# Single-query attention over 8192 keys: one loop over all pairs of heads on TensorE, VectorE and ScalarE

## Chip, cores and metric

The kernel runs on one core of a Trainium2 chip. The metric is device time in microseconds (us); lower is better. The time before is 321.45 us, the median of 3 runs (321.19 to 321.46).

## What is computed

Sixteen heads, one query per head, 8192 keys and values of 256 numbers each, all bf16. The softmax goes over the 8192 scores of a head.

```python
B, H, Sq, Sk, D = 1, 16, 1, 8192, 256
def reference(q, k, v):
    scale = q.shape[-1] ** -0.5
    scores = jnp.einsum("bhqd,bhkd->bhqk", q, k) * scale
    p = _softmax(scores, axis=-1)
    return jnp.einsum("bhqk,bhkd->bhqd", p, v)
```

## The kernel before

**Layout.** A head's K is 128 x 64 x 256: partition p holds keys 64p to 64p+63, as 64 columns of 256 numbers (`J` = 64). V lies the same way. One head of K or of V is 4096 KB. There are two buffers for K, two for V (`kbuf`, `vbuf`, by the parity of the head), and two each of scores `S`, exponents `E`, the query copy `q_now` and the accumulator `acc`.

**SyncE** (L124 to L140) issues all transfers from a list, in the order k(h+2), v(h), k(h+3), v(h+1) and so on. K of head h waits until VectorE (semaphore `kd`) and TensorE (`tp`) have read K of head h-2; V of head h waits for the products of head h-2 (`pv`). The first K comes in 16 and 48 columns; V of head 13 comes in halves, of head 14 in chunks of 16 columns, of head 15 in chunks of 16, 16, 12, 8, 6, 4 and 2 (`V_LATE`).

**VectorE** (L165) makes 48 of a head's 64 scores per partition, one multiply-and-add per column (`tensor_tensor_reduce`, L186). Then it takes the row maximum over all 64 columns, `m` (L203). In between it does two small steps for the head before: `xmax` (L169) reduces the 128 maxima, which TensorE has transposed into `mx`, to one number `g`; `recips` (L174) inverts the sum of exponents. `xmax` runs after column 11 (`xmax_at=11`). Head 0 and head 15 are written apart from the loop, and head 15 is called with `xmax_at=0`. A head starts when its K has landed, its query copy is there (`qb`), and the exponents of the head two back have been taken (`ex`).

**TensorE** (L214) makes the other 16 scores. `scores(t)` is, in this order: `transpose_m` of head t-1 (L218: row maxima to one row); four groups, each of `ktrans` (L278: 8 transposes of K to `tp`) and, one group later, `kscore` (L292: 8 products with the query, from the copy `KT` that ScalarE makes of `tp`); after `ktrans` of group 1 and `kscore` of group 0, `bcast` of head t-1 (L224: `g` to all partitions, waits for VectorE's L169); at the end `total` of head t-1 (L234: sum of the exponents). `pv(h)` is 64 products of a column of exponents with a column of V (L244), summed in `acc`; I call it P·V. Outside the loop stand the scores of heads 0 and 1; the loop does scores(t), pv(t-2) for t = 2 to 15, two heads a turn; behind it `pv_late` does P·V of 14 and 15 chunk by chunk, and in that of 14 the three small matmuls of head 15 come after 32, 48 and 64 products.

**ScalarE** (L353) is unrolled over the heads. For head t: the result of head t-3 (`final`, L394, and the output transfer), four copies `KT` (L368), after the first of them the query copy of head t+1 (`q_copy`, L359), after the second `expo` of head t-1 (L376 negates the broadcast maximum, L380 takes the exponents), at the end `scopy` (L372: TensorE's scores to `S`).

**GpSimd** makes two identity matrices and two rows of ones at the start.

Every engine runs its instructions in order; the order above is the one written in the code. In a loop turn a semaphore's awaited value comes from the turn's number (`_Step.of`).

Of the kernel before, what the change touches and what calls it, by code (L numbers as in the profile page):

```python
# [15 lines left out]
V_LATE = {14: (16, 16, 16, 16), 15: (16, 16, 12, 8, 6, 4, 2)}  # L16


class _Step:
# [10 lines left out]
    def back(self, n):  # L30
        return _Step(self.c - n, self.i)
# [6 lines left out]
def bass_standalone__mha_softmax__decode_kernel(nc: bass.Bass, q: bass.AP, k: bass.AP, v: bass.AP, out: bass.AP):  # L38
# [15 lines left out]
    stream = [("k", 0, 0, K_FIRST, "k00"), ("k", 0, K_FIRST, J, "k0"), ("k", 1, 0, J, "k1")]  # L54
    stream += [("v", 0, 0, HALF, "va0"), ("k", 2, 0, J, "k0"), ("v", 0, HALF, J, "va0")]
    stream += [("v", 1, 0, HALF, "va1"), ("k", 3, 0, J, "k1"), ("v", 1, HALF, J, "va1")]
    for h in range(2, H):
        if h + 2 < H:
            stream.append(("k", h + 2, 0, J, f"k{h % 2}"))
        if h in V_LATE:  # L60
            c = 0
            for i, s in enumerate(V_LATE[h]):
                stream.append(("v", h, c, c + s, f"v{h}_{i}"))
                c += s
        elif h == V_HALVED:
            stream += [("v", h, 0, HALF, f"va{h % 2}"), ("v", h, HALF, J, f"vb{h % 2}")]
        else:
            stream.append(("v", h, 0, J, f"va{h % 2}"))

    with contextlib.ExitStack() as ctx:  # L70
# [17 lines left out]
        q_all = sb("q_all", [P, H * QW], dt)  # L88
# [24 lines left out]
        for name in ("l", "rc", "pv", "fin", "ldq", "k00", "k0", "k1", "va0", "va1", "vb0", "vb1", "o0", "o1"):  # L113
            sem(name)
        for h, sizes in V_LATE.items():
            for i in range(len(sizes)):
                sem(f"v{h}_{i}")
# [4 lines left out]
        if True:  # L122

            @(lambda f: f(nc.sync))  # L124
            def _(sp):
                for kind, h, a, b, name in stream:
                    buf = (kbuf if kind == "k" else vbuf)[h % 2]
                    if h >= 2 and a == 0:
                        if kind == "k":
                            sp.wait_ge(sem("kd"), h - 1)  # L130
                            sp.wait_ge(sem("tp"), (h - 1) * NG)
                        else:
                            sp.wait_ge(sem("pv"), h - 1)
                    sp.dma_start(  # L134
                        buf[:, a * D : b * D], src(k if kind == "k" else v, h)[:, a * D : b * D]
                    ).then_inc(sem(name), 16)
                    if kind == "v" and b == J and h not in V_LATE and h != V_HALVED:

                        sp.nop().then_inc(sem(f"vb{h % 2}"), 16)
# [3 lines left out]
            def _(pool):  # L143
# [19 lines left out]
                pool.memset(ones_col[:, :], 1.0).then_inc(sem("cf"), 1)  # L163

            @(lambda f: f(nc.vector))  # L165
            def _(dve):
                def xmax(h):
                    dve.wait_ge(sem("mT"), h.of(1, 1))
                    dve.tensor_reduce(g[0:1, h.par : h.par + 1], mx[0:1, 0:P], AX.X, ALU.max).then_inc(sem("g"), 1)  # L169

                def recips(h):
                    dve.wait_ge(sem("l"), h.of(1, 1))
                    dve.wait_ge(sem("fin"), h.of(1, 1))
                    dve.reciprocal(recip[0:1, h.par : h.par + 1], mx[0:1, P : P + 1]).then_inc(sem("rc"), 1)  # L174

                def head(h, first=False, xmax_at=11):
                    dve.wait_ge(sem("qb"), h.of(1, 1))
                    dve.wait_ge(sem("ex"), h.of(1, 0) if not first else 1)
                    buf = kbuf[h.par]
                    for j in range(JD):  # L180
                        if first and j == 0:
                            dve.wait_ge(sem("k00"), 16)
                        if j == (K_FIRST if first else 0):

                            dve.wait_ge(sem(f"k{h.par}"), h.of(8, 16 - 8 * h.par))  # L185
# [10 lines left out]
                        if j == xmax_at and not first:  # L196
                            xmax(h.back(1))
                    ins.then_inc(sem("kd"), 1)
                    if not first:
                        recips(h.back(1))  # L200
                    dve.wait_ge(sem("kd"), h.of(1, 1))
                    dve.wait_ge(sem("sc"), h.of(1, 1))
                    dve.tensor_reduce(m[:, h.par : h.par + 1], S[h.par][:, :], AX.X, ALU.max).then_inc(sem("m"), 1)  # L203
# [11 lines left out]
            def _(pe):  # L215
                def transpose_m(h):
                    pe.wait_ge(sem("m"), h.of(1, 1))
# [4 lines left out]
                def bcast(h):  # L222
                    pe.wait_ge(sem("g"), h.of(1, 1))
# [8 lines left out]
                def total(h):  # L232
                    pe.wait_ge(sem("ex"), h.of(1, 2))
                    pe.matmul(  # L234
                        mx[0:1, P : P + 1],
# [6 lines left out]
                def products(h, a, b):  # L242
                    for j in range(a, b):
# [7 lines left out]
                    if b == J:  # L251
                        ins.then_inc(sem("pv"), 1)

                def pv(h):
                    pe.wait_ge(sem("fin"), h.of(1, 1))

                    for a, name, more in ((0, "va", 16), (HALF, "vb", 0)):
                        pe.wait_ge(sem(f"{name}{h.par}"), h.of(8, 16 + more - 8 * h.par))
                        products(h, a, a + HALF)

                def pv_late(h, between):
                    pe.wait_ge(sem("fin"), h.of(1, 1))
                    a = 0
                    for i, s in enumerate(V_LATE[h.c]):
                        pe.wait_ge(sem(f"v{h.c}_{i}"), 16)
                        products(h, a, a + s)
                        a += s
                        if i in between:
                            between[i]()

                def ktrans(h, gi):
                    buf = kbuf[h.par]
                    if gi == 0:
                        pe.wait_ge(sem(f"k{h.par}"), h.of(8, 16 - 8 * h.par))
                    for b in range(GRP):
# [9 lines left out]
                def kscore(h, gi, first):  # L285
                    pe.wait_ge(sem("kt"), h.of(NG, gi + 1))
                    if gi == 0 and not first:
                        pe.wait_ge(sem("sc"), h.of(1, 0))
# [12 lines left out]
                def scores(t, first=False):  # L301
                    if not first:
                        transpose_m(t.back(1))
                    for gi in range(NG):
                        ktrans(t, gi)
                        if gi >= 1:
                            kscore(t, gi - 1, first)
                        if gi == 1 and not first:
                            bcast(t.back(1))
                    kscore(t, NG - 1, first)  # L310
                    if not first:
                        total(t.back(1))
# [25 lines left out]
                pe.wait_ge(sem("cf"), 3)  # L338
# [12 lines left out]
                pv_late(last, {})  # L351

            @(lambda f: f(nc.scalar))  # L353
            def _(act):
                def q_copy(h):
                    if h >= 2:
                        act.wait_ge(sem("kd"), h - 1)
                        act.wait_ge(sem("sp"), (h - 1) * NG)
                    act.activation(  # L359
                        out=q_now[h % 2][:, :], in_=q_all[:, h * QW : (h + 1) * QW], func=ACT.Copy  # L360
                    ).then_inc(sem("qb"), 1)

                def evac(h, gi):
                    n = h * NG + gi
                    act.wait_ge(sem("tp"), n + 1)
                    if n >= 2:
                        act.wait_ge(sem("sp"), n - 1)
                    act.activation(out=KT[gi % 2][:, :], in_=tp[gi % 2][:, :], func=ACT.Copy).then_inc(sem("kt"), 1)  # L368

                def scopy(h):  # L370
                    act.wait_ge(sem("sp"), (h + 1) * NG)
                    act.activation(out=S[h % 2][:, JD:J], in_=spe[:, 0:NPE], func=ACT.Copy).then_inc(sem("sc"), 1)  # L372

                def expo(h):
                    act.wait_ge(sem("bc"), h + 1)
                    act.activation(  # L376
                        out=negb[:, h % 2 : h % 2 + 1], in_=sm[:, 0:1], func=ACT.Copy, scale=-1.0
                    ).then_inc(sem("nb"), 1)
                    act.wait_ge(sem("nb"), h + 1)
                    act.activation(  # L380
                        out=E[h % 2][:, :],
                        in_=S[h % 2][:, :],
                        func=ACT.Exp,
                        bias=negb[:, h % 2 : h % 2 + 1],
                        scale=1.0,
                        accum_out=lsum[:, h % 2 : h % 2 + 1],
                    ).then_inc(sem("ex"), 1)

                def final(h):
                    act.wait_ge(sem("rc"), h + 1)  # L390
                    act.wait_ge(sem("pv"), h + 1)
                    if h >= 2:
                        act.wait_ge(sem(f"o{h % 2}"), 16 * (h // 2))
                    act.activation(  # L394
                        out=o_sb[h % 2][0:1, :],
                        in_=acc[h % 2][0:1, 0:D],
                        func=ACT.Copy,
                        scale=recip[0:1, h % 2 : h % 2 + 1],
                    ).then_inc(sem("fin"), 1)
                    act.wait_ge(sem("fin"), h + 3)  # L400
# [68 lines left out]
```

## Time and profile before

| | |
|---|---|
| median of 3 runs | 321.45 us |
| the profiled execution | 320.95 us |
| its span on the core | 319.5 us |
| VectorE busy | 274.4 us |
| TensorE matmuls busy | 225.7 us |
| ScalarE busy | 93.0 us |
| HBM read | 134.23 MB |
| mean granted TensorE clock | 0.829 |

All views below come from the profiled execution. PE is TensorE's matmuls, PEld its weight loads, DVE is VectorE, ACT ScalarE, POOL GpSimd, SPq the queue of SyncE. A row of the timeline has the start in us from the span's start, the length, the engine, the line (L186 is line 186 of the kernel before), the instruction, out<-in, how many stand in the row, and in brackets the engine's idle time before and what ended it. A row of a table of stretches has the stretch, its length, busy time of each engine with the number of instructions, then the granted clock (1.00 is full), the mean busy share of the 16 DMA engines, and GB/s. Where one line stands out of its view, "..." is above or below it.

### The profile page before, as it was taken

What the parts mean: (1) busy time and instruction counts of PE and PEld (TensorE: products, weight loads), DVE (VectorE), ACT (ScalarE), POOL (GpSimd) and SP (SyncE); (2) the same over time, 40 slices, a digit from 0 to 9 for tenths busy, and PEclk for the clock granted to TensorE, in tenths of its full rate; (3) what the DMA queues carried; (4) which work ended last, traced back from release to release, by engine and by line L of the source; (5) the groups of instructions that cost most, each with busy time, mean ns of one, the idle gap of its engine ahead of it and who ended that gap; (6) DMA issues with size and microseconds to landing.
All of it is one profiled execution on the core that took longest, in us unless ns stands there. A gap on an engine that the chain in (4) does not pass through costs nothing.

```text
span 319.5 us, 6525 instructions
## 1 busy us (share of the span) xinstructions
PE 225.7 (71%) x2162; PEld 161.9 (51%) x2162; DVE 274.4 (86%) x1584; ACT 93.0 (29%) x170; POOL 1.3 (0%) x10
## 2 busy tenths in 40 slices
PE   3627059788795958668585793957759577597997
PEld 1325045556564645546454563744546445465774
DVE  1999999999999999797997979989797997969910
ACT  4525132333315060330603314042330603305010
POOL 1000000000000000000000000000000000000000
PEclk9999999969687885969669597885957859697899
DMA  8999999999999999999999999999999999999994
GB/s 329 451 401 443 401 457 412 406 438 435 423 451 410 443 439 423 435 419 451 414 443 435 423 443 410 451 424 431 439 419 451 414 439 439 419 418 418 424 415 183
DMA packets 6553, 134.34 MB, mean 421 GB/s; under 512 B 752, under 2 KB 912, under 8 KB 1424
## 3 DMA queue, kind: packets, MB, share of 16 engines
q1 hardware_dynamic: 6480, 134.22, 98.3%
q8 instruction: 4, 0.07, 0.1%
q14 instruction: 5, 0.04, 0.0%
q10 hardware_dynamic: 64, 0.02, 0.0%
HBM read 134.23 MB, written 0.01 MB: 420 GB/s over the span
## 4 chain that ended last, share of the span: by engine, by line
DVE 50%; DMA 40%; PE 5%; issue 3%; ACT 1%; DVEq 0%; SPq 0%; ACTq 0%
DVE kbuf L186 48%; DMA kbuf<-in_k_dram 37%; PE acc L244 5%; DMA vbuf<-in_v_dram 3%; DVE S L186 2%; ACT KT L368 1%; DVE g L169 1%; SPq L134 0%; PE tp L278 0%; ACT o_sb L394 0%; PE spe L292 0%; DVE recip L174 0%; DVEq L206 0%; DVEq L185 0%; ACT E L380 0%
## 5 line engine op out<-in xcount | busy, mean ns | idle before, releaser
L186 DVE CUSTOM_DVE_ANT_0 kbuf<-kbuf,q_now 128x256 bf16<-128x256 bf16 x768 | 267.8, 411 | 30.2 <-DMA kbuf<-in_k_dram 22.4
L244 PE MATMUL acc<-vbuf,E 128*1 128x256 bf16 x1024 | 146.1, 315 | 14.5 <-DMA vbuf<-in_v_dram 14.4
L244 PEld LDWEIGHTS acc<-vbuf,E 128*1 128x1 bf16 x1024 | 97.4, 96 | 59.7 <-issue 14.9
L368 ACT ACTIVATE KT<-tp 128x1024 bf16<-128x1024 bf16 x64 | 64.4, 1020 | 30.4 <-PE tp L278 30.0
L186 DVE DVE_READ_ACCUMULATOR2_ANT S<- 128x1 f32 x768 | 56.4, 73 | 0.0
L394 ACT ACTIVATE o_sb<-acc,recip 1x256 bf16<-1x256 f32 x16 | 7.4, 464 | 153.5 <-PE acc L244 152.3
L278 PE MATMUL tp<-identb,kbuf 128*128 128x128 bf16 x512 | 46.2, 252 | 5.6 <-DMA kbuf<-in_k_dram 5.6
L278 PEld LDWEIGHTS tp<-identb,kbuf 128*128 128x128 bf16 x512 | 36.3, 113 | 10.4 <-DMA kbuf<-in_k_dram 5.3
L292 PE MATMUL spe<-q_now,KT 128*128 128x1 bf16 x512 | 23.6, 167 | 24.0 <-ACT KT L368 23.6
L292 PEld LDWEIGHTS spe<-q_now,KT 128*128 128x128 bf16 x512 | 19.4, 104 | 32.1 <-ACT KT L368 32.1
L224 PE MATMUL sm<-g,ones_row 1*128 1x1 f32 x32 | 7.1, 288 | 28.1 <-DVE g L169 28.1
L224 PEld LDWEIGHTS sm<-g,ones_row 1*128 1x128 f32 x32 | 5.7, 221 | 29.6 <-DVE g L169 29.3
L218 PE MATMUL mx<-ident,m 128*1 128x128 f32 x32 | 6.5, 288 | 13.9 <-DVE m L203 13.9
L376 ACT ACTIVATE negb<-sm 128x1 f32<-128x1 f32 x16 | 2.7, 172 | 28.9 <-PE sm L224 28.9
L218 PEld LDWEIGHTS mx<-ident,m 128*1 128x1 f32 x32 | 2.5, 84 | 14.8 <-DVE m L203 14.1
L359 ACT ACTIVATE q_now<-q_all 128x258 bf16<-128x258 bf16 x16 | 6.5, 410 | 0.0
L329 PE MATMUL acc<-q_sb,identb 16*128 16x256 bf16 x16 | 4.4, 403 | 2.3 <-ACT q_all L415 2.3
L169 DVE TENSOR_REDUCE g<-mx 1x1 f32<-1x128 f32 x16 | 4.4, 274 | 1.9 <-PE mx L218 1.9
L380 ACT ACTIVATE E<-S,negb 128x64 bf16<-128x64 f32 x16 | 5.6, 348 | 0.5
L174 DVE RECIPROCAL recip<-mx 1x1 f32<-1x1 f32 x16 | 2.4, 152 | 3.7 <-PE mx L234 3.7
L372 ACT ACTIVATE S<-spe 128x16 f32<-128x16 f32 x16 | 2.9, 183 | 7.5 <-PE spe L292 7.5
L415 ACT ACTIVATE q_all<-acc 128x512 bf16<-128x512 f32 x8 | 4.4, 592 | 0.6 <-PE acc L329 0.6
(19 smaller groups left out, 15.7 us busy)
## 6 DMA issues: line engine op xcount, KB each, us to landing
kbuf<-in_k_dram SPq DMA_DIRECT2D x15, 4096.0 KB, 21.9
vbuf<-in_v_dram SPq DMA_DIRECT2D x11, 4096.0 KB, 29.2
vbuf<-in_v_dram SPq DMA_DIRECT2D x6, 2048.0 KB, 24.0
vbuf<-in_v_dram SPq DMA_DIRECT2D x6, 1024.0 KB, 14.6
kbuf<-in_k_dram SPq DMA_DIRECT2D x1, 3072.0 KB, 11.6
kbuf<-in_k_dram SPq DMA_DIRECT2D x1, 1024.0 KB, 4.7
vbuf<-in_v_dram SPq DMA_DIRECT2D x1, 768.0 KB, 10.9
vbuf<-in_v_dram SPq DMA_DIRECT2D x1, 512.0 KB, 11.7
```

What stands on the lines that cost most here:

```text
L169: dve.tensor_reduce(g[0:1, h.par : h.par + 1], mx[0:1, 0:P], AX.X, ALU.max).then_inc(sem("g"), 1)
L186: ins = dve.tensor_tensor_reduce(out=buf[:, j * D : (j + 1) * D], in0=buf[:, j * D : (j + 1) * D], in1=q_now[h.par][:, 0:D], scale=SCALE, ...
L218: pe.matmul(mx[0:1, 0:P], lhsT=m[:, h.par : h.par + 1], rhs=ident[:, :], start=True, stop=True).then_inc(sem("mT"), 1)
L224: pe.matmul(sm[:, 0:1], lhsT=ones_row[0:1, 0:P], rhs=g[0:1, h.par : h.par + 1], start=True, stop=True,).then_inc(sem("bc"), 1)
L244: ins = pe.matmul(acc[h.par][0:1, 0:D], lhsT=E[h.par][:, j : j + 1], rhs=vbuf[h.par][:, j * D : (j + 1) * D], start=(j == 0), stop=(j == J ...
L278: ins = pe.transpose(tp[gi % 2][:, b * D + hf * P : b * D + (hf + 1) * P], buf[:, j * D + hf * P : j * D + (hf + 1) * P], identb[:, :],)
L292: ins = pe.matmul(spe[:, c : c + 1], lhsT=KT[gi % 2][:, b * D + hf * P : b * D + (hf + 1) * P], rhs=q_now[h.par][:, D + hf : D + hf + 1], ...
L329: ins = pe.matmul(acc[pair % 2][:, (h % 2) * D : (h % 2 + 1) * D], lhsT=identb[0:H, h : h + 1].to_broadcast([H, P]), rhs=q_sb[:, :], start ...
L359: act.activation(out=q_now[h % 2][:, :], in_=q_all[:, h * QW : (h + 1) * QW], func=ACT.Copy).then_inc(sem("qb"), 1)
L368: act.activation(out=KT[gi % 2][:, :], in_=tp[gi % 2][:, :], func=ACT.Copy).then_inc(sem("kt"), 1)
L380: act.activation(out=E[h % 2][:, :], in_=S[h % 2][:, :], func=ACT.Exp, bias=negb[:, h % 2 : h % 2 + 1], scale=1.0, accum_out=lsum[:, h % 2 ...
L394: act.activation(out=o_sb[h % 2][0:1, :], in_=acc[h % 2][0:1, 0:D], func=ACT.Copy, scale=recip[0:1, h % 2 : h % 2 + 1],).then_inc(sem("fin ...
```

## The change

The three engines get one loop each, over all eight pairs of heads (TensorE has nine turns). What the first and last turns lack or need is told by branches on the turn's number and by semaphores that GpSimd counts up at the start (`AHEAD`, and 16 or 32 on some of the transfers' semaphores). `ev` and `od` are the even and odd head of a turn, `old` or `prev` is the odd head of the turn before.

- VectorE: head `ev` runs `xmax` of `prev` after column 40; head `od` runs `recips` of `prev` after column 8, `xmax` of `ev` after column 11 and `recips` of `ev` at its end. What concerns `prev` stands in a branch. There is no head written apart.
- TensorE: a turn is scores(ev) without the small matmuls, P·V of the even head of the turn before with the small matmuls of `old` after 32, 48 and 64 products, scores(od) with those of `ev`, P·V of `old`. Each part stands in a branch. Every P·V has the waits at the chunk borders of heads 14 and 15; the value awaited rises with the last turn. `total` writes to `qps` in place of `mx`.
- ScalarE: a loop of eight turns with two heads. `expo` of the odd head of the turn before comes behind `scopy` of the even head; `final` of head t-2 comes at the end of head t, in a branch. `q_copy` copies head t+1 for all t, so for a head 16 too, whose query is set to zero (`q_all` is longer by one head). `expo` of 15 and `final` of 14 and 15 stand behind the loop.
- SyncE: the same transfers in the same order; awaited values are shifted by what is counted up, and the no-ops behind whole V transfers go.

```diff
+AHEAD = {"kd": 1, "sc": 1, "sp": 2, "ex": 2, "m": 1, "g": 1, "mT": 1, "l": 1, "bc": 1, "nb": 1, "rc": 2, "pv": 2, "fin": 4}
+V_SEMS = (("va0", "v0b", "v0c", "v0d"), ("va1", "v1b", "v1c", "v1d", "v1e", "v1f", "v1g"))
...
                         if kind == "k":
-                            sp.wait_ge(sem("kd"), h - 1)
+                            sp.wait_ge(sem("kd"), h)
                             sp.wait_ge(sem("tp"), (h - 1) * NG)
                         else:
-                            sp.wait_ge(sem("pv"), h - 1)
+                            sp.wait_ge(sem("pv"), h + 1)
...
-                        sp.nop().then_inc(sem(f"vb{h % 2}"), 16)
...
+                pool.memset(q_all[:, H * QW : (H + 1) * QW], 0.0).then_inc(sem("cf"), 1)
+                for name, n in AHEAD.items():
+                    pool.nop().then_inc(sem(name), n)
...
-                head(_Step(0), first=True)
-                with dve.Fori(0, (H - 2) // 2) as i:
-                    head(_Step(1, i))
-                    head(_Step(2, i))
+                with dve.Fori(0, H // 2) as i:
+                    ev, od = _Step(0, i), _Step(1, i)
+                    prev = od.back(2)
+
+                    def later(f):
+                        with dve.If(i > 0):
+                            f(prev)
+
+                    head(ev, {40: lambda: later(xmax)})
+                    head(od, {8: lambda: later(recips), 11: lambda: xmax(ev), JD: lambda: recips(ev)})
                 last = _Step(H - 1)
-                head(last, xmax_at=0)
                 xmax(last)
                 recips(last)
...
-                scores(_Step(0), first=True)
-                scores(_Step(1))
-                with pe.Fori(0, (H - 2) // 2) as i:
-                    for c in (2, 3):
-                        t = _Step(c, i)
-                        scores(t)
-                        pv(t.back(2))
-                last = _Step(H - 1)
-                pv_late(
-                    last.back(1),
-                    {1: lambda: transpose_m(last), 2: lambda: bcast(last), 3: lambda: total(last)},
-                )
-                pv_late(last, {})
+                with pe.Fori(0, H // 2 + 1) as i:
+                    ev, od = _Step(0, i), _Step(1, i)
+                    fin_turn = pe.snap((i // 8) * 16 + 16)
+                    half_turn = pe.snap(((i + 1) // 8) * 16 + 16)
+                    old = od.back(2)
+                    with pe.If(i < H // 2):
+                        scores(ev)
+                    with pe.If(i > 0):
+                        pv(
+                            ev.back(2),
+                            {V_LATE[14][n]: [(V_SEMS[0][n], fin_turn)] for n in range(1, len(V_SEMS[0]))},
+                            {32: lambda: transpose_m(old), 48: lambda: bcast(old), 64: lambda: total(old)},
+                        )
+                    with pe.If(i < H // 2):
+                        scores(od, before=ev)
+                    with pe.If(i > 0):
+                        waits = {V_LATE[15][n]: [(V_SEMS[1][n], fin_turn)] for n in range(1, len(V_SEMS[1]))}
+                        waits[HALF].append(("v1h", half_turn))
+                        pv(old, waits, {})
...
-                for t in range(H):
-                    if t >= 3:
-                        final(t - 3)
-                    for gi in range(NG):
-                        evac(t, gi)
-                        if gi == 1 and t >= 1:
-                            expo(t - 1)
-                        if gi == 0 and 1 <= t < H - 1:
-                            q_copy(t + 1)
-                    scopy(t)
-                final(H - 3)
-                expo(H - 1)
-                final(H - 2)
-                final(H - 1)
+                with act.Fori(0, H // 2) as i:
+                    for c in (0, 1):
+                        t = _Step(c, i)
+                        evac(t, 0)
+                        act.wait_ge(sem("kd"), t.of(1, 1))
+                        act.wait_ge(sem("sp"), t.of(NG, 2))
+                        q_copy(_Step(c + 1, i), q_all[:, bass.ds(i * (2 * QW) + (c + 1) * QW, QW)])
+                        evac(t, 1)
+                        if c:
+                            expo(t.back(1))
+                        evac(t, 2)
+                        evac(t, 3)
+                        scopy(t)
+                        with act.If(i > 0):
+                            if c == 0:
+                                expo(t.back(1))
...
+                            final(done, flat[:, bass.ds(at, D)])
+                expo(_Step(H - 1))
+                for h in (H - 2, H - 1):
+                    final(_Step(h), out[0, h, 0:1, :])
```

More of the change, by code (lines that the diff above doesn't have):

```diff
@@ L112, in bass_standalone__mha_softmax__decode_kernel @@
             sem(name)
-        for name in ("l", "rc", "pv", "fin", "ldq", "k00", "k0", "k1", "va0", "va1", "vb0", "vb1", "o0", "o1"):
+        for name in ("l", "rc", "pv", "fin", "ldq", "k0", "k0b", "k1", "va0", "va1", "v1h", "o0", "o1"):
             sem(name)
-        for h, sizes in V_LATE.items():
-            for i in range(len(sizes)):
-                sem(f"v{h}_{i}")
+        late = [name for row in V_SEMS for name in row[1:] if name not in ("v0c", "v1c")] + ["v1h"]
+        for row in V_SEMS:
+            for name in row[1:]:
+                sem(name)
         def src(t, h):
@@ L167, in xmax, with head @@
                 def xmax(h):
-                    dve.wait_ge(sem("mT"), h.of(1, 1))
+                    dve.wait_ge(sem("mT"), h.of(1, 2))
                     dve.tensor_reduce(g[0:1, h.par : h.par + 1], mx[0:1, 0:P], AX.X, ALU.max).then_inc(sem("g"), 1)
                 def recips(h):
[L172 to L176, printed above, removed]
+                    dve.wait_ge(sem("l"), h.of(1, 2))
+                    dve.wait_ge(sem("fin"), h.of(1, 3))
+                    dve.reciprocal(recip[0:1, h.par : h.par + 1], qps[0:1, 0:1]).then_inc(sem("rc"), 1)
+                def head(h, at):
                     dve.wait_ge(sem("qb"), h.of(1, 1))
-                    dve.wait_ge(sem("ex"), h.of(1, 0) if not first else 1)
+                    dve.wait_ge(sem("ex"), h.of(1, 1))
+                    dve.wait_ge(sem(f"k{h.par}"), h.of(8, 16 - 8 * h.par))
                     buf = kbuf[h.par]
                     for j in range(JD):
[L181 to L185, printed above, removed]
+                        if j == K_FIRST and h.par == 0:
+                            dve.wait_ge(sem("k0b"), 16)
                         ins = dve.tensor_tensor_reduce(
@@ L195, in head @@
                         )
-                        if j == xmax_at and not first:
-                            xmax(h.back(1))
+                        if j in at:
+                            at[j]()
                     ins.then_inc(sem("kd"), 1)
[L199 to L202, printed above, removed]
+                    if JD in at:
+                        at[JD]()
+                    dve.wait_ge(sem("kd"), h.of(1, 2))
+                    dve.wait_ge(sem("sc"), h.of(1, 2))
                     dve.tensor_reduce(m[:, h.par : h.par + 1], S[h.par][:, :], AX.X, ALU.max).then_inc(sem("m"), 1)
-                head(_Step(0), first=True)
-                with dve.Fori(0, (H - 2) // 2) as i:
-                    head(_Step(1, i))
-                    head(_Step(2, i))
+                with dve.Fori(0, H // 2) as i:
[6 more added lines that the diff above has]
+                    head(od, {8: lambda: later(recips), 11: lambda: xmax(ev), JD: lambda: recips(ev)})
                 last = _Step(H - 1)
-                head(last, xmax_at=0)
                 xmax(last)
@@ L240, in total, with pv @@
                     ).then_inc(sem("l"), 1)
-                def products(h, a, b):
-                    for j in range(a, b):
+                def pv(h, waits, at):
+                    pe.wait_ge(sem("fin"), h.of(1, 3))
+                    pe.wait_ge(sem(f"va{h.par}"), h.of(8, 32 - 8 * h.par))
+                    for j in range(J):
+                        for name, value in waits.get(j, ()):
+                            pe.wait_ge(sem(name), value)
                         ins = pe.matmul(
@@ L250, in products @@
                         )
[L251 to L269, printed above, removed]
+                        if j == J - 1:
+                            ins.then_inc(sem("pv"), 1)
+                        if j + 1 in at:
+                            at[j + 1]()
                 def ktrans(h, gi):
@@ L283, in ktrans, with kscore @@
                     ins.then_inc(sem("tp"), 1)
-                def kscore(h, gi, first):
+                def kscore(h, gi):
                     pe.wait_ge(sem("kt"), h.of(NG, gi + 1))
-                    if gi == 0 and not first:
-                        pe.wait_ge(sem("sc"), h.of(1, 0))
+                    if gi == 0:
+                        pe.wait_ge(sem("sc"), h.of(1, 1))
                     for b in range(GRP):
@@ L299, in kscore, with scores @@
                     ins.then_inc(sem("sp"), 1)
-                def scores(t, first=False):
-                    if not first:
-                        transpose_m(t.back(1))
+                def scores(t, before=None):
+                    if before:
+                        transpose_m(before)
                     for gi in range(NG):
@@ L306, in scores @@
                         if gi >= 1:
[L307 to L312, printed above, removed]
+                            kscore(t, gi - 1)
+                        if gi == 1 and before:
+                            bcast(before)
+                    kscore(t, NG - 1)
+                    if before:
+                        total(before)
                 pe.wait_ge(sem("ldq"), 16)
@@ L353, in _, with q_copy @@
             @(lambda f: f(nc.scalar))
             def _(act):
[L355 to L361, printed above, removed]
+                def q_copy(h, src_q):
+                    act.activation(out=q_now[h.par][:, :], in_=src_q, func=ACT.Copy).then_inc(sem("qb"), 1)
@@ L411, in _ @@
                     scale=SCALE,
-                ).then_inc(sem("fin"), 2)
+                )
                 for pair in range(H // 2):
```

93 lines of the change are left out of this document (49 added, 44 removed).

## The prediction

> **What bounds the kernel now.** First the page: engines, DMA row, queue row.
>
> ```profile
> span 319.5 us, 6525 instructions
> PE 225.7 (71%) x2162; PEld 161.9 (51%) x2162; DVE 274.4 (86%) x1584; ACT 93.0 (29%) x170; POOL 1.3 (0%) x10
> ...
> DMA  8999999999999999999999999999999999999994
> q1 hardware_dynamic: 6480, 134.22, 98.3%
> ```
>
> The 16 DMA engines are full from the second slice to the last but one; no compute engine is. K and V together are 134.22 MB, and one queue carries them. A delay on TensorE, VectorE or ScalarE therefore costs nothing until it either empties the queue (a buffer freed too late) or lies behind the last bytes. Second view: the chain of work that ended last, cut to the end of the span (start, length, what).
>
> ```profile
> 264.95 21.94 DMA kbuf<-in_k_dram
> ...
> 286.94 0.64 PE tp L278 x8
> ...
> 292.55 9.77 PE acc L244 x64
> ...
> 302.71 9.47 DMA vbuf<-in_v_dram
> ...
> 312.22 5.59 PE acc L244 x48
> ...
> 317.89 0.46 ACT o_sb L394
> ```
>
> The last K (head 15) lands at 264.95 + 21.94 = 286.89. From there TensorE is in the chain almost to the end: scores of head 15, P·V of head 13 (x64, ends at 302.32), P·V of 14 and 15. It meets the V stream again only at 312.18, when a chunk of V of head 15 lands; the 48 products left then end at 317.81. So at the end TensorE has hardly anything to spare: whatever makes the scores of head 15 end later is late for three heads of products in a row.
>
> Third view: how long scores take, by the timeline of TensorE and VectorE (start, length, what, idle before it and its releaser) for heads 14 and 15.
>
> ```profile
> 267.50 0.42 DVE L186 CUSTOM_DVE_ANT_0 kbuf<-kbuf,q_now 128x256 bf16<-128x256 bf16 x1 [2.31 <-DMA kbuf<-in_k_dram]
> ...
> 271.65 0.27 DVE L169 TENSOR_REDUCE g<-mx 1x1 f32<-1x128 f32 x1
> ...
> 271.98 0.38 PE L224 MATMUL sm<-g,ones_row 1*128 1x1 f32 x2 [1.74 <-DVE g L169]
> ...
> 275.25 0.19 PE L234 MATMUL mx<-ones_col,lsum 128*1 128x1 f32 x2
> ...
> 287.06 0.42 DVE L186 CUSTOM_DVE_ANT_0 kbuf<-kbuf,q_now 128x256 bf16<-128x256 bf16 x1 [2.43 <-DMA kbuf<-in_k_dram]
> ...
> 287.41 0.28 DVE L169 TENSOR_REDUCE g<-mx 1x1 f32<-1x128 f32 x1
> ...
> 288.96 0.38 PE L224 MATMUL sm<-g,ones_row 1*128 1x1 f32 x2
> ...
> 292.25 0.19 PE L234 MATMUL mx<-ones_col,lsum 128*1 128x1 f32 x2
> ```
>
> In head 14, VectorE reduces the maximum of the head before (L169) after twelve dot products, 4.15 us after its first; TensorE's broadcast (L224) stands waiting for it 1.74 us, and the scores end (L234) 7.75 us after VectorE's start. In head 15 the kernel before passes xmax_at=0: L169 runs after one dot product, the broadcast waits for nothing, and L234 comes 5.19 us after VectorE's start. The short form is worth 2.56 us, and it stands at the one head where TensorE's time counts.
>
> **The change, part by part.**
>
> *The special last head goes.* VectorE's loop now has all 16 heads, and an odd head runs xmax of the even one at j = 11. So in head 15 the broadcast waits as in head 14. VectorE's start there is unchanged at 287.06 (below); one reciprocal more, of the head two back, comes ahead of it at j = 8 and takes the place of 0.1 us. L234 comes at 287.06 + 7.75 + 0.1 = 294.9 and ends at 295.1; ScalarE's extra q_copy of a head 16 that does not exist is inside the 7.75, since head 14 has one. Products of head 13 start 0.1 us later (292.44 to 292.55 before): 295.2 instead of 292.55, 2.65 us late.
>
> *What becomes of these 2.65 us* depends on the speed of the products (L244 alone in four stretches: length, PE busy, count; then the granted clock), and on the 64 products of other heads:
>
> ```profile
> 277.30:280.90 3.60, 3.58 (x18) 2.13 (x19) 0.51 1.01 437
> ...
> 292.50:297.90 5.40, 5.35 (x26) 3.25 (x27) 0.50 0.99 417
> 297.90:305.60 7.70, 7.70 (x72) 5.86 (x70) 1.00 1.01 421
> ```
>
> ```profile
> 257.88 10.02 PE L244 MATMUL acc<-vbuf,E 128*1 128x256 bf16 x64 [1.77 <-DMA vbuf<-in_v_dram]
> ...
> 277.32 8.86 PE L244 MATMUL acc<-vbuf,E 128*1 128x256 bf16 x64 [1.89 <-DMA vbuf<-in_v_dram]
> ```
>
> A product costs 7.70/72 = 0.107 us at clock 1.00 and 5.40/26 = 0.208 at 0.50. P·V of 12 and of 13 begin at half clock and turn full on the way. With that of 11, P·V of a head took 10.02, 8.86 and 9.77 us. I take 9.5 for head 13, near their mean: 304.7 (302.32 before). Then P·V of 14 with the three small matmuls of head 15 in it, which the new code has at the same places (after 32, 48, 64 products): before, from 302.32 to the end of its last 16,
>
> ```profile
> 308.00 1.91 PE L244 MATMUL acc<-vbuf,E 128*1 128x256 bf16 x16
> ```
>
> 309.91, 7.6 us: now 312.3. The V chunks of head 15 that held TensorE until 312.18 have by then landed, and the slack ahead of them is used up; 64 products at 0.107 to 5.59/48 = 0.116 are 6.9 to 7.4, I take 7.2: **319.5 instead of 317.8, 1.7 us later.** ScalarE's final and the output transfer follow as before. Bounds: 8.86 for head 13 and 6.9 for 15 give 318.5 (+0.7); 10.02, 7.4, and 0.7 for a late VectorE and for jumps give 320.9 (+3.1).
>
> *Statistics of odd heads move.* transpose, broadcast and total of head 2i-1 leave the scores of 2i and go into P·V of 2i-2, after 32, 48 and 64 products; xmax goes to j = 40 of the even head, expo behind scopy. VectorE may now wait at j = 40, and behind it stand seven dot products, the reduction m, the free-signal of K and head 2i+1. In head 14 VectorE is there at 267.50 + 41 x 0.346 (4.15/12) = 281.7. P·V of 12 begins at 277.32; its first 18 products take 3.6 us, 14 more 1.5; transpose 0.4: VectorE waits until 282.8, 1.1 us. Its reduction m stood here:
>
> ```profile
> 284.41 0.22 DVE L203 TENSOR_REDUCE m<-S 128x1 f32<-128x64 f32 x1
> ```
>
> It moves to 285.6 and is still 1.2 us ahead of K's landing at 286.89: nothing. The same holds in each even head past the sixth, with at most 32 x 0.208 = 6.7 us of products, a wait of 2.7 and 0.1 to 0.4 us of late start. The exponent that head 15 waits for (S buffer) comes after product 48, near 285.7: also in time. Cover: VectorE's own wait for K, 2.31 and 2.43 us in the rows above.
>
> *K and V buffers.* SyncE's list of transfers is the same, and so are the heads it waits for; some no-ops go. What counts is when K is issued, against the end of what is queued ahead. VectorE frees it:
>
> ```profile
> 23.99 0.33 SPq L134 DMA_DIRECT2D kbuf<-in_k_dram  x1
> ...
> 58.54 0.33 SPq L134 DMA_DIRECT2D kbuf<-in_k_dram  x1
> ...
> 128.94 0.33 SPq L134 DMA_DIRECT2D kbuf<-in_k_dram  x1
> ...
> 10.00:60.00 50.00, 27.56 (x272) 20.76 (x270) 48.41 (x280) 15.21 (x25) 0.00 (x0) 1.00 1.00 428
> ```
>
> Ahead of the issue at 23.99 lie 10 x 1.049 MB, of that at 58.54 24 x 1.049 MB: at 428 GB/s, from some 1.2 us on, they last to 25.7 and 60.0 at the earliest. So at least 1.5 us are spare early. Later more: K of head 15 takes 21.94 us from issue to landing, and 4.19 MB alone take 9.8, so 12 us lie ahead of it. VectorE loses in the first heads what the branches cost, and nothing else: it runs behind K there, so xmax at j = 40 finds its input.
>
> *Loops and branches.* A jump back on VectorE is in the trace: between m and the next head's first dot product lie 0.75 us with it and 0.29 without.
>
> ```profile
> 58.54 0.22 DVE L203 TENSOR_REDUCE m<-S 128x1 f32<-128x64 f32 x1
> 59.29 0.43 DVE L186 CUSTOM_DVE_ANT_0 kbuf<-kbuf,q_now 128x256 bf16<-128x256 bf16 x1 [0.53 <-issue]
> ...
> 41.34 0.22 DVE L203 TENSOR_REDUCE m<-S 128x1 f32<-128x64 f32 x1
> 41.63 0.42 DVE L186 CUSTOM_DVE_ANT_0 kbuf<-kbuf,q_now 128x256 bf16<-128x256 bf16 x1
> ```
>
> That is 0.46 us. A branch that is passed or jumped over is bounded by 0 and 0.46; inside a head, with queued work in front of it, I take 0; two in a turn are at most 0.9 of the 2.31 + 2.43 us that VectorE waits for K in a turn. On TensorE they follow queued matmuls, on ScalarE (29% busy) hundreds of us of idle time: 0. GpSimd's no-ops that pre-count the semaphores come after its 1.3 us of work and must be through when VectorE first waits for ScalarE, at 6.4 us: 0.
>
> **Sum.** 320.95 is the profiled execution's own time, 1.45 around its span; plus 1.7 it is 322.65. The runs' median, 321.45, is 0.5 above it: **323.1 us**, 0.5% slower. A measurement of this kernel can tell about 0.2%, 0.64 us, from no change.
>
> **Rivals.**
>
> *A, not slower: products of head 13 at full clock.* The mechanism is the same, but if they begin at 295.2 without half clock, they end at 295.2 + 64 x 0.107 + 0.3 = 302.3, as now, and everything behind them is as before: 321.4. It decides below about 2.3 us at half clock: each costs 1 - 0.107/0.208 = 0.49 us, some 0.5 are spare ahead of 312.22 (309.91 and 16 products make 311.7), and 0.64 are not told from no change. Against it stand the stretches of the whole kernel in head 14, whose scores look like the new ones:
>
> ```profile
> 267.40:275.50 8.10, 4.51 (x75) 3.55 (x72) 8.00 (x46) 5.31 (x10) 0.00 (x0) 0.91 1.04 449
> 275.50:277.30 1.80, 0.00 (x0) 0.01 (x1) 1.80 (x11) 0.04 (x1) 0.00 (x0) 0.50 0.76 328
> ```
>
> A mean of 0.91 is some 1.5 of the 8.1 us at 0.50: the clock falls inside the scores, though TensorE's one long wait there was 1.74 us. The Trainium skill, "TensorE: Matmul & The Clock Gate", Part 1: The HAM clock gate, has the clock fall only after an idle window of about 3.4 us; by that rule scores with a 1.7 us wait would leave it full and A would hold, but this trace shows it fall. For A: when the clock turns is not tied to the program. Chance 0.14.
>
> *B, the code is fetched again at jumps.* The trace has few fetches:
>
> ```profile
> q8 instruction: 4, 0.07, 0.1%
> q14 instruction: 5, 0.04, 0.0%
> ```
>
> The Trainium skill, "Runtime: NRT & Kernel Launch", Instruction fetch mechanics, says that a taken branch to a target outside two pages stalls on a fetch. Here the loops of before made no more than these fetches; 0.1% of 16 engines' span over 4 packets is 1.3 us each. One on TensorE at its last turn, between P·V of 13 and 14, adds up to 1.3: 324.4. Chance 0.10.
>
> *C, the queue runs dry early.* If VectorE loses over 1.5 to 4 us in heads 0 to 2, K comes late and the loss adds to the end, some 2 us: 325. Chance 0.07.
>
> *D, faster.* ScalarE's and VectorE's shorter code spares fetches; 0.11 MB are 0.3 us of the queue. With A it gives 321.0. Chance 0.05.
>
> **Chances.** Forecast 0.64, A 0.14, B 0.10, C 0.07, D 0.05. Slower by over 0.2%: forecast but for its lowest edge (0.04), B and C: 0.77; within: 0.18; faster: 0.05. The range runs from A's side, 321.8, over the forecast's bounds (322.1 to 324.5) to B and part of C, 325.0.
>
> **What would show it.** Right: VectorE's g in head 15 near 291.4 and TensorE's broadcast right behind it; last scores end near 295; products of 15 without a wait for V, ending near 319.5; queue rows as now; VectorE waiting for mx at j = 40 in even heads. Wrong: broadcast in head 15 not held up; products of 13 mostly at 1.00; a gap in the DMA row; more instruction packets than nine.

## The result, and the profile after

The changed kernel takes 322.75 us (median of 6 runs, 321.76 to 323.51) against 321.16 for the kernel before (6 runs, 321.0 to 321.46): ratio 1.0046, 95% interval 1.0036 to 1.0056. It is slower by 1.6 us, and the forecast was 1.65. The profiled execution took 321.76, the fastest of the six; the spread of the runs, 1.75 us against 0.46 before, is part of the story.

The page of the changed kernel, the same rows as before and the two for code:

```profile
span 320.3 us, 6845 instructions
...
DMA  8999999999999999999999999999999999999994
...
q1 hardware_dynamic: 6480, 134.22, 98.1%
q8 instruction: 2, 0.03, 0.0%
...
q14 instruction: 3, 0.02, 0.0%
```

The queue is as full as before up to the last heads, and there are fewer code packets, five in place of nine. So neither rival B nor C. Only near 304 us, where V of head 15 is issued behind the late products of head 13, the DMA engines' share is 0.63 to 0.82 for 1.5 us; TensorE never waits for that V. The chain of work that ended last, from the last K on (line numbers are those of the changed kernel: 189 the dot products, 173 xmax, 226, 232 and 242 the three small matmuls, 257 the products):

```profile
264.90 21.74 DMA kbuf<-in_k_dram
...
291.10 0.21 DVE g L173
291.31 0.04 issue
291.36 0.48 PE sm L232 x2
...
295.48 11.99 PE acc L257 x96
...
311.61 7.02 PE acc L257 x64
...
318.70 0.47 ACT o_sb L392
```

Between the last K and the end no transfer of V stands in the chain any more. VectorE's maximum stands there instead, then the broadcast, then three heads of products without a pause. TensorE's timeline shows the wait, and where the products of head 13 and of head 15 begin (the row of 96 holds the 64 products of head 13 and the first 32 of head 14):

```profile
291.36 0.48 PE L232 MATMUL sm<-g,ones_row 1*128 1x1 f32 x2 [1.88 <-DVE g L173]
...
295.29 0.19 PE L242 MATMUL qps<-ones_col,lsum 128*1 128x1 f32 x2
295.43 12.04 PE L257 MATMUL acc<-vbuf,E 128*1 128x256 bf16 x96
...
311.47 7.15 PE L257 MATMUL acc<-vbuf,E 128*1 128x256 bf16 x64
```

The products of head 13 begin at 295.43 (292.55 before), those of head 15 at 311.47, and they end at 318.62 (317.81 before). These 0.8 us are what the profiled execution lost (321.76 against 320.95); the slowest of the six lost 2.6 against the same 320.95.

### The profile page after: what moved, and what is told of

Same layout as the page of the kernel before. It is cut to its first block, busy times and chain, and to the rows that moved or that the text cites. A ratio compares the mean times of both kernels' runs of the same rounds, so it can differ in the third digit from the quotient of the medians.

```text
span 320.3 us, 6845 instructions
## 1 busy us (share of the span) xinstructions
PE 223.4 (70%) x2162; PEld 159.4 (50%) x2162; DVE 274.7 (86%) x1584; ACT 94.1 (29%) x171; POOL 1.6 (0%) x11
## 4 chain that ended last, share of the span: by engine, by line
DVE 51%; DMA 37%; PE 8%; issue 2%; ACT 1%; DVEq 0%; SPq 0%; ACTq 0%
DVE kbuf L189 48%; DMA kbuf<-in_k_dram 37%; PE acc L257 7%; DVE S L189 2%; DVE g L173 1%; PE tp L278 1%; ACT KT L367 0%; PE sm L232 0%; PE spe L292 0%; DVE recip L178 0%; ACT o_sb L392 0%; ACT q_now L362 0%; SPq L136 0%; DVEq L183 0%; PE mx L226 0%
## 5 line engine op out<-in xcount | busy, mean ns | idle before, releaser
L257 PEld LDWEIGHTS acc<-vbuf,E 128*1 128x1 bf16 x1024 | 95.7, 95 | 68.4 <-DMA vbuf<-in_v_dram 26.1
L189 DVE DVE_READ_ACCUMULATOR2_ANT S<- 128x1 f32 x768 | 58.8, 77 | 0.0
L292 PEld LDWEIGHTS spe<-q_now,KT 128*128 128x128 bf16 x512 | 18.6, 102 | 38.8 <-ACT KT L367 28.6
L362 ACT ACTIVATE q_now<-q_all 128x258 bf16 (+1 forms) x17 | 7.0, 413 | 0.2 <-DVE S L189 0.2
L178 DVE RECIPROCAL recip<-qps 1x1 f32<-1x1 f32 x16 | 2.4, 150 | 3.7 <-PE qps L242 3.7
```

What stands on the lines that cost most here:

```text
L189: ins = dve.tensor_tensor_reduce(out=buf[:, j * D : (j + 1) * D], in0=buf[:, j * D : (j + 1) * D], in1=q_now[h.par][:, 0:D], scale=SCALE, ...
L257: ins = pe.matmul(acc[h.par][0:1, 0:D], lhsT=E[h.par][:, j : j + 1], rhs=vbuf[h.par][:, j * D : (j + 1) * D], start=(j == 0), stop=(j == J ...
L292: ins = pe.matmul(spe[:, c : c + 1], lhsT=KT[gi % 2][:, b * D + hf * P : b * D + (hf + 1) * P], rhs=q_now[h.par][:, D + hf : D + hf + 1], ...
L362: act.activation(out=q_now[h.par][:, :], in_=src_q, func=ACT.Copy).then_inc(sem("qb"), 1)
```

## The experiments

The theory: in head 15 the broadcast waits for VectorE's twelfth dot product, and TensorE is then late to the end. The main rival: the loops, branches and moved statistics cost the time. The four kernels b_last11, a_od0, b_last23 and a_ev30 ran beside the kernel before at 321.34 (18 runs), the four others at 321.3 (29 runs).

**b_last11: this part alone, in the kernel before.**

```diff
-                head(last, xmax_at=0)
+                head(last, xmax_at=11)
```

> The kernel before with one number changed: in head 15 the maximum of head 14 is reduced after twelve dot products, as in every other head, not after one. No new loop, no branch, no moved statistics. Theory (the broadcast in the scores of head 15 waits for VectorE, and TensorE is late for three heads of products): products of head 13 begin near 295.1 in place of 292.55, 322.6 us (321.8 to 323.4). Rival (loops, branches and moved statistics cost the time): within 0.3 us of before, 321.2.

Measured: 323.12 us (321.56 to 323.47), ratio 1.0047 (1.003 to 1.0064). One number gives the whole loss, without a loop or a branch. TensorE's timeline:

```profile
291.50 0.38 PE L224 MATMUL sm<-g,ones_row 1*128 1x1 f32 x2 [2.11 <-DVE g L169]
...
294.81 13.04 PE L244 MATMUL acc<-vbuf,E 128*1 128x256 bf16 x96
...
311.85 7.17 PE L244 MATMUL acc<-vbuf,E 128*1 128x256 bf16 x64
```

The broadcast waits 2.11 us, and the two groups of products begin at the changed kernel's times within 0.7 us.

**a_od0: the change without this part.**

```diff
-                    head(od, {8: lambda: later(recips), 11: lambda: xmax(ev), JD: lambda: recips(ev)})
+                    head(od, {0: lambda: (later(recips), xmax(ev)), JD: lambda: recips(ev)})
```

> The changed kernel, with the two small VectorE steps of odd heads moved from after dot products 9 and 12 to after the first; loops, branches and everything else stay. Theory: scores of head 15 end some 5.5 us after its K lands, products of head 13 begin near 292.7, the end is set by the last V again: 321.2 us (320.8 to 321.6). Rival (loops, branches, moved statistics): it stays with the changed kernel, 322.4 to 323.

Measured: 320.67 us (320.27 to 322.77, 12 runs), ratio 0.9985 (0.9972 to 0.9998). With all its loops, branches and moved statistics the kernel is not slower than before, if anything a little faster. TensorE's timeline:

```profile
289.72 0.38 PE L232 MATMUL sm<-g,ones_row 1*128 1x1 f32 x2
...
293.50 13.40 PE L257 MATMUL acc<-vbuf,E 128*1 128x256 bf16 x96
...
310.91 7.15 PE L257 MATMUL acc<-vbuf,E 128*1 128x256 bf16 x64
```

No wait stands at the broadcast. The products of head 13 begin at 293.50, 0.8 later than expected, and TensorE still has all 64 products of head 15 ahead of it at 310.91: here too it sets the end in the profiled execution. The 0.8 us are the rest of the change at this place. The chain ahead of the scores of head 15 no longer comes from K:

```profile
247.29 29.44 DMA vbuf<-in_v_dram
276.77 6.25 PE acc L257 x32
283.24 1.74 PE acc L257 x16
285.30 1.85 PE acc L257 x16
```

It runs over V of head 12 and its products, which now hold the three small matmuls of head 13 and end at 287.15, after K of head 15 has landed. ScalarE adds to it: its first copy of K comes behind the result of head 12 (TensorE waits 1.03 us for it, 0.67 before), and the query copy of the head 16 that does not exist (0.41 us) stands ahead of the second. So the changed code does cost some tenths of a microsecond here, but not the loss, and the main rival falls.

**b_last23: twice the delay.**

```diff
-                head(last, xmax_at=0)
+                head(last, xmax_at=23)
```

> The kernel before with the maximum of head 14 reduced after 24 dot products of head 15: twice the suspected delay. Theory: products of head 13 begin near 299.1 (4.15 us after those with twelve) and all of it arrives at the end, 326.4 us (325.2 to 327.5). Rival (slack behind the scores takes it up, the end hangs on V and VectorE): under 323.

Measured: 326.83 us (326.28 to 327.54), ratio 1.0183 (1.017 to 1.0196).

```profile
295.57 0.58 PE L224 MATMUL sm<-g,ones_row 1*128 1x1 f32 x2 [6.42 <-DVE g L169]
...
299.66 12.14 PE L244 MATMUL acc<-vbuf,E 128*1 128x256 bf16 x96
```

Twelve more dot products (4.15 us) move the start of the products by 4.85 us, from 294.81 to 299.66, and the time by 3.7. The start moves by more than 4.15 because the clock is at half when the broadcast comes: the transposes behind it take 1.03 us in place of 0.62. The time moves by less, for 0.9 us come back in the products themselves, 12.14 us for 96 in place of 13.04, although TensorE has rested three times as long. Nothing behind the scores takes up the delay.

**a_ev30: the moved wait of even heads, made longer.**

```diff
-                    head(ev, {40: lambda: later(xmax)})
+                    head(ev, {30: lambda: later(xmax)})
```

> The changed kernel with the other moved wait made longer: in even heads VectorE waits for TensorE's transpose after dot product 31, not 41, so 3.46 us earlier and that much longer (some 4.7 us in head 14). If the wait after 41 is hidden by VectorE's wait for K with about 0.8 us to spare, as the theory has it, head 15 now starts some 2.5 us late and the time is near 325 us (323.8 to 326). Rival 1 (the wait is on the path as it stands): 3.5 more than the changed kernel, 326.2. Rival 2 (VectorE is never on the path): 322.7.

Measured: 325.0 us (324.12 to 325.99), ratio 1.0115 (1.0097 to 1.0133), 2.25 above the changed kernel. First the rows of VectorE around head 14's end in the changed kernel, then those of this one:

```profile
282.97 0.28 DVE L173 TENSOR_REDUCE g<-mx 1x1 f32<-1x128 f32 x1 [1.46 <-PE mx L226]
...
285.69 0.22 DVE L206 TENSOR_REDUCE m<-S 128x1 f32<-128x64 f32 x1
286.81 0.43 DVE L189 CUSTOM_DVE_ANT_0 kbuf<-kbuf,q_now 128x256 bf16<-128x256 bf16 x1 [0.90 <-DMA kbuf<-in_k_dram]
```

```profile
283.46 0.28 DVE L173 TENSOR_REDUCE g<-mx 1x1 f32<-1x128 f32 x1 [3.41 <-PE mx L226]
...
289.64 0.22 DVE L206 TENSOR_REDUCE m<-S 128x1 f32<-128x64 f32 x1
289.79 0.43 DVE L189 CUSTOM_DVE_ANT_0 kbuf<-kbuf,q_now 128x256 bf16<-128x256 bf16 x1
```

The changed kernel waits 1.46 us for the transpose and then still 0.90 for K: the wait is paid out of time that VectorE has. With a wait of 3.41 us and seventeen dot products behind it in place of seven, K is no longer waited for, and head 15 begins at 289.79, 3 us later. (The wait had been expected at 4.7 us: VectorE comes to it only 1.5 us earlier than in the changed kernel, not 3.46, since it began head 14 2 us later, at 269.24 in place of 267.24.) So the moved wait is free where it stands, with under a microsecond to spare in head 14.

**a_warm: the clock.**

```diff
+                            for _ in range(16):
+                                pe.matmul(
+                                    sm[0:1, 256 : 256 + D],
+                                    lhsT=identb[:, 0:1],
+                                    rhs=q_all[:, 0:D],
+                                    start=True,
+                                    stop=True,
+                                )
                             bcast(before)
```

> The changed kernel with 16 more matmuls of the shape of the products, on data that nothing uses, ahead of the broadcast in the scores of odd heads, where TensorE waits 1.9 us for VectorE in head 15. Theory on the clock (products of head 13 are slow because TensorE rests in the scores, so their length depends on how much it rested): the wait filled, the 64 products of head 13 take near 7.2 us in place of 8.4, and the time falls by 1 to 2 us, to 321.3 (320.8 to 322.0). Rival (the half clock comes anyway, or the matmuls themselves are late): 322.5 to 324.

Measured: 321.29 us (320.06 to 322.64, 12 runs), ratio to before 0.9999 (0.9983 to 1.0015). The change's loss is gone, though the broadcast comes no earlier (291.88, against 291.36). The products alone in two stretches of head 13, first in the changed kernel, then here (length, PE busy and count, PEld, granted clock, DMA, GB/s):

```profile
295.40:298.60 3.20, 3.17 (x17) 1.92 (x18) 0.54 0.98 407
298.60:303.70 5.10, 5.10 (x49) 3.92 (x47) 1.00 1.01 422
```

```profile
295.20:298.60 3.40, 3.31 (x31) 2.56 (x32) 1.00 1.01 422
298.60:302.40 3.80, 3.80 (x38) 2.92 (x36) 1.00 1.00 418
```

Seventeen products in 3.2 us at 0.54 against 31 in 3.4 us at 1.00. So the products of head 13 begin slow because TensorE has rested in the scores ahead of them; with the rest filled, the clock stays full. But the change did not bring this. In the kernel before, too, the clock falls in the scores of head 15, where TensorE never waits longer than 0.67 us. From tables of stretches 0.1 us long, all times in us:

| | at half clock | head 13's products begin | of them at half clock | row of 96 products |
|---|---|---|---|---|
| before | 291.1 to 297.9 | 292.55 | 5.4 | 13.25 |
| a_od0 | 292.4 to 299.2 | 293.50 | 5.7 | 13.40 |
| b_last11 | 292.9 to 299.7 | 294.81 | 4.9 | 13.04 |
| changed | 291.5 to 298.3 | 295.43 | 2.9 | 12.04 |
| b_last23 | 292.5 to 302.7 | 299.66 | 3.0 | 12.14 |
| a_warm | never | 295.29 | 0 | 10.64 |

The slow stretch begins in the scores with the long wait and without it. It lasts 6.8 us in four of these executions and 10.2 in b_last23, and the later the products begin, the more of it has passed. So in these profiles half clock is no part of what the change costs; fewer products at half clock gave back 1.2 of the 2.9 us of late start in the changed kernel. What a_warm takes out is another loss of about the same size, which was there before the change as well. Against the changed kernel run beside it (a_again, 322.26) a_warm gains 1.0 us, against the first result 1.5. Its runs still spread over 2.6 us; what the slow ones lack was not profiled.

**a_od0_warm: both.** As a_od0, with 6, 4 and 4 idle matmuls ahead of three waits for ScalarE's copies:

```diff
+                        if before and gi in (1, 3):
+                            pe.wait_ge(sem("sc"), t.of(1, 1))
+                            keep_busy(6 if gi == 1 else 4)
                         if gi >= 1:
                             kscore(t, gi - 1)
...
+                    if before:
+                        keep_busy(4)
                     kscore(t, NG - 1)
```

> The changed kernel with the odd heads' VectorE steps after the first dot product, and 6, 4 and 4 idle matmuls of the products' shape in the three waits for ScalarE's copies in the scores of odd heads. Theory: head 13's products run near full clock, TensorE catches up with V, the end hangs on the last V alone, 320.2 us (319.9 to 320.6), 0.4 under the version without these matmuls. Rival (rest in the scores does not set the clock): 320.7 or, if they delay the scores, 321.3.

Measured: 320.58 us (320.08 to 321.39), ratio 0.9978 (0.9969 to 0.9988): clearly under the kernel before, but not told apart from a_od0. The chain shows what was expected of it:

```profile
293.43 7.14 PE acc L257 x64
...
300.95 10.24 DMA vbuf<-in_v_dram
...
311.23 1.91 PE acc L257 x16
```

The 64 products of head 13 take 7.14 us, and V of head 15 stands in the chain again. With TensorE caught up, the last V sets the end of this execution, and from there a faster TensorE has little more to give. The expected 0.4 us against a_od0 did not show in the medians, so it is the trace, not the time, that speaks for the theory on the clock here.

**a_od0_b and a_again: second profiles.** Kernels a_od0 and the changed one, unaltered.

> The changed kernel with the odd heads' VectorE steps after the first dot product once more, beside the version with idle matmuls: 320.7 us, and a second profile. If the end hangs on TensorE in it, its span goes with the length of head 13's products.

> The changed kernel unaltered, for a second profile. Theory: its runs differ by up to 1.75 us because the stretch at half clock falls differently on head 13's products; span less their length is the same as in the first profile (320.3 less 8.4) within 0.3 us. Rival: the difference lies in the transfers, and the last V lands later by it.

Measured: 320.49 us (320.27 to 322.97, 7 runs; ratio 0.9982, 0.9967 to 0.9996) and 322.26 us (321.57 to 323.72, 10 runs; ratio 1.0038, 1.0025 to 1.0051). The profiled execution of a_od0_b took 322.97 us, and not for the reason expected: its products of head 13 with the first half of 14 take 13.54 us, hardly longer than in the first profile (13.40). They begin at 295.13, 1.6 us later, because the transfers were late: V of head 12 landed at 278.18 (248.96 + 29.22), in a_od0 at 276.73 (it was issued 1.7 us later, and took as long). The chain of a_od0_b up to the scores of head 15:

```profile
248.96 29.22 DMA vbuf<-in_v_dram
278.21 6.48 PE acc L257 x32
...
288.99 0.47 ACT o_sb L392
```

So some of the spread lies in the transfers. What held them up in this one execution was not found. In a_again the same 96 products take 12.37 us (12.04 in the first profile) and the span is 320.5 (320.3): less those products 308.1 and 308.3, as expected, but two profiles so alike settle little about the spread. All profiles together say where to look: in the eight in which TensorE does not wait for V of head 15, its last product ends 11.15 to 11.37 us after the row of 96 does. What differs between executions is when that row begins and how much of the half clock falls on it.

## Why the prediction was right

**Short and long scores.** The price of xmax at j = 11 in head 15, 2.56 us and 0.1 for the reciprocal, put the start of head 13's products at 295.2; it was 295.43. That it came so near is in part luck: VectorE began head 15 0.25 us earlier than before (286.81), and the scores behind the broadcast took 3.93 us to the start of the last small matmul, at half clock, in place of 3.27 in head 14. b_last11 and a_od0 show this to be the cause, one by adding it and one by taking it away.

**Nothing else takes it up.** Shown by b_last23. The slack ahead of 312.22 was used up, as forecast: no wait for V is left in the chain. With the last 48 products a little faster it was worth 0.85 us, where some 0.5 were forecast.

**Products of head 13.** This is the term that was mis-sized. I took 9.5 us. In the profiled execution the 96 products of head 13 and of the first half of 14 end at 295.43 + 12.04 = 307.47, and 32 of them at full clock are 3.4 us: those of head 13 end near 304.0 and took 8.6, a little below the 8.86 of my lower bound. That is why this execution lost only 0.8 us. I took the mean length of earlier heads and did not ask how much of the slow stretch is over when the products begin late. The rows of the kernel before could have told: had it ended at 297.9 again, products from 295.2 on would have had 2.7 us of it and taken some 8.2 us. The rest came as forecast: 7.6 us to the end of 14's products at 311.6 (7.6), then 7.0 (7.2). For the profiled execution the sum gave 322.65, 0.9 above the 321.76 that it took. The median lies a microsecond above the profiled execution, near the forecast, but what makes those other executions longer is not shown. So the wait is the shown cause of the loss, while the agreement of 1.65 with 1.6 us is luck in part.

**Rival A** had the right quantity, the clock at the start of head 13's products. Its condition did not come about by itself (0.54 in the first 3.2 us), and a_warm, which brings it about, lands at 321.3, where A put it (321.4). The rule of the Trainium skill weighed there ("TensorE: Matmul & The Clock Gate", Part 1: The HAM clock gate) has the clock fall after an idle window of about 3.4 us. These traces do not need so long a wait: TensorE's longest in these scores was 1.88 us, in those of the kernel before 0.67 us, and the clock fell in both. Shorter rests were enough here.

**Moved statistics: nothing.** The wait at j = 40 was 1.46 us (1.1 forecast), and 0.90 us of wait for K was left behind it (1.2 forecast). a_ev30 shows the edge near. In head 12 it was nearer: a wait of 2.10 us left 0.25 of wait for K in the changed kernel, and 2.29 us left none in a_again; VectorE's next wait, 2.1 us for K of head 14, took that up. I had it in every even head past the sixth; the table of waits has it in six heads:

```profile
DVE g L173 <- PE mx L226: 10.8, 6, 3.7
```

**Loops and branches: nothing, or a gain.** a_od0 has them all and is 0.67 us under before, 0.15% with an interval that ends just under 1. In its place I had named rival D, fewer code fetches, with 0.3 us. The last K does land 0.25 us earlier in the changed kernel (264.90 + 21.74 = 286.64 against 286.89), but that the four missing packets are the cause was only argued. Where the 0.67 us come from is open: the profiled execution of a_od0, 321.20, is one of its slower ones, and its last product ends no earlier than in the kernel before (318.06, 317.81).

## What to carry to other kernels

A kernel that is bound by its transfers can still lose time in the last heads, where no later transfer hides a delay: look there first for what a uniform loop takes away, since a special case at the end of a loop may be the one place where the order counts. Look also at the granted clock ahead of the final work: here that work began at half clock with the delay and without it, and filling a rest in front of it won back as much as the delay had cost. How much a delay costs then depends on how much of the slow stretch it lets pass, so one profile gives its cause but not its size. Here the uniform loop and the early maximum go together, and that version (320.5 to 320.7 us) is about 2 us under the changed kernel and 0.7 to 0.8 under the one before, the latter with intervals that end just under a ratio of 1.

## What was not expected of the hardware

Sixteen matmuls whose result nobody reads, put in a wait of 1.88 us, made the work behind them faster: 10.64 us for 96 products in place of 12.04, because the granted clock stayed at 1.00, and 1.0 to 1.5 us in the median (321.29 against 322.26 and 322.75). The wait itself need not be long for the clock to fall: it fell in the kernel before behind waits of at most 0.67 us. And a branch on VectorE cost nothing where work was queued ahead of it. The chain of the changed kernel shows the reciprocal of odd heads, which stands in a branch after dot product 9, without a gap on either side:

```profile
289.66 0.34 DVE kbuf L189
290.01 0.07 DVE recip L178
290.08 0.32 DVE kbuf L189
```
